# Strided value tiles loaded as 128 rows instead of 118 in a fused attention and feed-forward kernel

## The chip, the cores and the metric

The kernel runs on one core of a Trainium2 chip. Its time is device microseconds of one execution. Before the change three runs gave 945.47, 946.59 and 947.21 us, a median of 946.59 us. The profiled execution took 947.53 us; its span from the first to the last instruction is 945.7 us. All times below are counted from the start of that span.

## The reference

Attention with 8 heads over 8 sequences of 576 positions, then a feed-forward block on all 4608 tokens. Heads 0 to 3 see the last 32 keys (local), heads 4 to 7 see every 32nd key (strided):

```python
rel = pos[:, None] - pos[None, :]
mask_local = (rel >= 0) & (rel < stride)                      # stride = 32
mask_strided = (rel >= 0) & (pos[None, :] % stride == pos[:, None] % stride)
...
attn = softmax(where(mask, q @ k.T / 8, -1e9));  x = attn @ v
h = x @ w_in                                                  # 512 -> 2048
g = h * (1.0 / (1.0 + np.exp(-1.702 * h)))
return g @ w_out                                              # 2048 -> 512
```

## The kernel before

The host lays the inputs out, the core does the rest. Attention goes in 42 units, which the code calls pairs: 18 local ones (kind "l", 256 tokens each) and 24 strided ones (kind "s", eight sequences times three groups of residues). Each unit has two loads. `load_qk` (L132) brings queries and keys into a tile `qk`, of which there are two buffers. `load_v` (L140) brings values into a tile `v`, of which there are also two buffers: for a local unit 96 rows of 4096 bytes, for a strided one 118 rows of 2048 bytes. In the strided tile rows 0 to 53 are the keys of one half, rows 64 to 117 those of the other; ten rows between them are zero.

A unit then goes through six steps on the engines: `scores` (TensorE; on the trace `s` or `u`, with a small matmul from `masks_sb` ahead), `maxima` (VectorE, `nmax`), the exponentials of `softmax` (ScalarE, `pr`) and their scaling (VectorE `rinv`, GpSimd `pr`), the transposition of the probabilities (in the first nine units by TensorE into `t`, `turn_pr`, and VectorE copies into `pt_l` or `pt_s`, `fetch_pt`), `values` (TensorE, `a`, which reads `pt` and `v`), and the split of the result into a high and a low part (ScalarE `xhl`/`xhs`, VectorE `xll`/`xls`).

The feed-forward block takes 384 tokens at a time, 12 groups; each has 16 steps over slices of the hidden width. A step is 12 matmuls into `h`, an activation (`g`, `gh`, `gl`) and nine matmuls into `o`. Weights come as `raw` (two loads of 512 KB a slice) and are split by ScalarE and VectorE into `w`.

The first nine units (`n0`), numbered 0 to 8 as l, l, s, s, s, s, l, s, s, come ahead of the feed-forward steps, in the loop of L607: turn i issues the scores of unit i+1, the exponentials of unit i, the values of unit i-2 and the transposition of unit i-1. The six strided ones are the units 2, 3, 4, 5, 7, 8. The other 33 units are woven into the feed-forward steps.

The order on each engine is that of the program here. SyncE (SP) issues all loads and stores, in one queue. `load_v(i)` in turn i stands behind the values of unit i-2, whose buffer it takes; weights of the first slices stand behind it (L625, and `load_w` in L449). Each of SP's loads also waits for the load eight places ahead of it, whose semaphore it takes over.

The tracer gives nearly all instructions L116, the line of a helper, so they are told apart by tile names.

Of the kernel before, what the change touches and what calls it, by code (L numbers as in the profile page):

```python
# [18 lines left out]
P = 128  # L19
B, H, S, D = 8, 8, 576, 64  # L20
# [4 lines left out]
QB = 64  # L25
KB = QB + STRIDE
RB = 3
NB = RB * NPOS
U = 2
# [3 lines left out]
NR = (12, 10, 10)  # L33
# [14 lines left out]
HEADS = 4  # L48
# [34 lines left out]
def attn_ffn(ctx, tc, lqk, sqk, lv, sv, w_in, w_out, masks, ident, out):  # L83
# [22 lines left out]
    class InOrder:  # L106
# [17 lines left out]
    vector, scalar, gpsimd, sync = (  # L124
        InOrder(e, strict) for e in (nc.vector, nc.scalar, nc.gpsimd, nc.sync)
    )
# [3 lines left out]
    qks, vts, banks, nmaxs, exps = {}, {}, {}, {}, {}  # L130
# [9 lines left out]
    def load_v(p):  # L140
        if p < len(pairs) and p not in vts:
            kind, a, c = pairs[p]
            vts[p] = io.tile([P, 2 * U * HEADS * D], F32, tag="v", name=f"v_{p}", bufs=2)
            if kind == "l":
                sync.dma_start(out=vts[p][:KB], in_=lv[a])
            else:
                n = U * HEADS * D
                sync.dma_start(out=vts[p][: QB + NB, :n], in_=sv[a * len(NR) + c])

    warm = const.tile([P, 1], F32, name="warm")  # L150
    vector.memset(warm, 0.0)
# [428 lines left out]
    steps = [(j, f) for j, f0, f1 in spans for f in range(f0, f1)]  # L580
    load_qk(1)
    load_v(0)
    ident_sb = const.tile([P, P], F32, name="ident_sb")
    sync.dma_start(out=ident_sb, in_=ident)
# [6 lines left out]
    maxima(0)  # L591
    load_qk(2)
    load_v(1)
    load_w(0)
    halfway, valued = {}, {}
# [11 lines left out]
    for i in range(n0):  # L607
        if i + 1 < n0:
            scores(i + 1)
            load_qk(i + 3)  # L610
        if i >= 1:
            scaled(i - 1)
        if i >= 2:
            fetch_pt(i - 2)
        if i >= 3:
            late_part(i - 3)
        if i + 1 < n0:
            maxima(i + 1)
        halfway[i] = softmax(i)
        run(halfway[i], 4)  # L620
        if i >= 2:
            value_products(i - 2)
            load_v(i)
            run(valued[i - 2], 1)
        if i % 2 and i // 2 + 1 < RAWB:  # L625
            load_w(i // 2 + 1)
        weigh(i and i + 1)
        if i == n0 - 2:
            turn_pr(i - 1)
            ffn1(*steps[0], (0, 1))  # L630
        elif i == n0 - 1:
            ffn1(*steps[0], (2, 3))
            turn_pr(i - 1)
        elif i >= 1:
            turn_pr(i - 1)
# [6 lines left out]
    p = n0  # L642
# [13 lines left out]
    for s in range(len(steps) + LAG):  # L656
# [3 lines left out]
        p, q, r = due.get(s), due.get(s - 1), begins.get(s)  # L660
# [46 lines left out]
def _layout(q, k, v, w_in, w_out):  # L707
    hl = H // 2
    pad = np.zeros((B, hl, STRIDE, D), np.float32)
    kp, vp = (np.concatenate([pad, x[:, :hl]], axis=2) for x in (k, v))  # L710
    nb = S // QB

    lqk = np.zeros((NP, 2, D, 2, QKW[0] // 2), np.float32)
    lv = np.zeros((NP, KB, 2 * U, HEADS, D), np.float32)
    for i in range(NP):
        for m in range(2 * U):
            b, n = divmod(2 * U * i + m, nb)
            u, g = divmod(m, 2)
            rows = q[b, :hl, n * QB : (n + 1) * QB]
            keys = kp[b, :, n * QB : n * QB + KB]  # L720
            at = u * 2 * QB + g * QB
            lqk[i, :, :, :, at : at + QB] = rows.reshape(2, 2, QB, D).transpose(1, 3, 0, 2)
            at = QW[0] + u * (KB + QB) + g * QB
            skip = STRIDE if g and not n else 0
            lqk[i, :, :, :, at + skip : at + KB] = keys[:, skip:].reshape(
                2, 2, KB - skip, D
            ).transpose(1, 3, 0, 2)
            lv[i, :, m] = vp[b, :, n * QB : n * QB + KB].transpose(1, 0, 2)

    ns = B * len(NR)  # L730
    sqk = np.zeros((ns, 2, D, 2, QKW[1] // 2), np.float32)
    sv = np.zeros((ns, QB + NB, U, HEADS, D), np.float32)
    for i in range(ns):
        b, c = divmod(i, len(NR))
        for m in range(2 * U):
            g, u = divmod(m, U)
            r0, r1 = R0[c] + RB * m, R0[c] + min(RB * (m + 1), NR[c])
            n = (r1 - r0) * NPOS
            x = [
                y[b, hl:].reshape(hl, NPOS, STRIDE, D)[:, :, r0:r1].transpose(0, 2, 1, 3).reshape(hl, n, D)  # L740
                for y in (q, k, v)
            ]
            at = u * (NB + QB) + g * NB
            sqk[i, :, :, :, at : at + n] = x[0].reshape(2, 2, n, D).transpose(1, 3, 0, 2)
            at = QW[1] + u * 2 * NB + g * NB
            sqk[i, :, :, :, at : at + n] = x[1].reshape(2, 2, n, D).transpose(1, 3, 0, 2)
            sv[i, g * QB : g * QB + n, u] = x[2].transpose(1, 0, 2)
    lqk, sqk = (x.reshape(len(x), P, -1) for x in (lqk, sqk))
    lv, sv = (x.reshape(*x.shape[:2], -1) for x in (lv, sv))

    wi = w_in.reshape(NC, P, NF, P).transpose(2, 1, 0, 3).reshape(NF, P, DM)
    wo = w_out.reshape(NF, P, DM)
    wi, wo = (np.ascontiguousarray(x).view(np.uint64) for x in (wi, wo))
    return lqk, sqk, lv, sv, wi, wo
# [43 lines left out]
```

## Time and profile before

| | before |
|---|---|
| runs (us) | 945.47, 946.59, 947.21 |
| profiled execution / its span (us) | 947.53 / 945.7 |
| TensorE matmul busy | 913.9 us, 97% |
| VectorE / ScalarE / GpSimd busy | 476.1 / 380.6 / 53.0 us |
| DMA: moved / mean rate | 62.08 MB / 66 GB/s |
| loads of strided values | 24 of 236 KB |
| loads of strided queries and keys | 24 of 452 KB |
| loads of weights | 32 of 512 KB, two a slice |

A row of the timeline gives the start and the length of a group of instructions, then engine, operation, tile written and tiles read, how many there are, and in brackets how long the engine had been idle before it and what ended that. A row of the windows gives for a stretch the busy time of each engine, TensorE's granted clock as a share of 2.4 GHz, the mean busy share of the 16 DMA engines and their rate.

### The profile page before, as it was taken

How to read it: one execution, taken by the hardware profiler on the slowest of the kernel's cores; microseconds unless marked ns; L12 is line 12 of the kernel's file. 1: busy time of each engine (PE TensorE's matmuls, PEld its weight loads, DVE VectorE, ACT ScalarE, POOL GpSimd, SP SyncE). 2: the span in 40 equal slices, each digit the busy share in tenths (PEclk: the TensorE clock that was granted, in tenths of full speed). 3: DMA queues.
4: the chain of work that ended last, by engine and by line, in shares of the span. 5: the costliest groups of instructions: out<-in, count | busy, mean ns of one | idle time of the engine just before them, and what ended most of it. 6: DMA issues, size and time to landing. Idle time of an engine off the chain costs nothing.

```text
span 945.7 us, 16069 instructions
## 1 busy us (share of the span) xinstructions
PE 913.9 (97%) x6432; PEld 806.6 (85%) x6432; DVE 476.1 (50%) x986; ACT 380.6 (40%) x1193; POOL 53.0 (6%) x50
## 2 busy tenths in 40 slices
PE   6569999999999999999999999999999999999998
PEld 4457888888888888888888888888888888898997
DVE  3648656565454663443655564453446565322322
ACT  5649755243433442423444333332433443222221
POOL 3100001010000100000000000000000010000000
PEclk6779999999999999999999999999999999999999
DMA  8659202112112111101212120110201310000000
GB/s 262 197 164 348 97 1 90 60 41 96 35 42 84 53 53 51 45 1 64 72 50 72 52 57 34 53 38 20 80 31 43 105 29 1 34 1 1 34 1 33
DMA packets 21242, 62.08 MB, mean 66 GB/s; under 512 B 2144, under 2 KB 2400, under 8 KB 21168
## 3 DMA queue, kind: packets, MB, share of 16 engines
q1 hardware_dynamic: 21168, 61.06, 19.7%
q8 instruction: 50, 0.82, 0.4%
q14 instruction: 24, 0.20, 0.1%
HBM read 51.62 MB, written 9.44 MB: 65 GB/s over the span
## 4 chain that ended last, share of the span: by engine, by line
PE 92%; DMA 7%; DVE 0%; issue 0%; SPq 0%; ACT 0%; DVEq 0%; ACTq 0%
PE o L116 43%; PE h L116 41%; PE a L116 4%; DMA v<-sv 4%; PE s L116 3%; DMA raw<-w_out 1%; DMA qk<-sqk 1%; DMA qk<-lqk 1%; PE u L116 0%; PE t L116 0%; SPq L116 0%; ACT raw L116 0%; DVE raw L116 0%; DVE w L116 0%; DVE out L116 0%
## 5 line engine op out<-in xcount | busy, mean ns | idle before, releaser
L116 PE MATMUL o<-w,gh 128*128 128x512 f32 x1152 | 307.6, 398 | 0.0
L116 PEld LDWEIGHTS o<-w,gh 128*128 128x128 f32 x1152 | 211.1, 187 | 39.0 <-ACT gh L116 0.4
L116 PE MATMUL h<-xhl,w 128*128 128x384 f32 x768 | 229.7, 339 | 2.0 <-DVE w L116 1.4
L116 PE MATMUL h<-xhs,w 128*128 128x384 f32 x768 | 227.2, 336 | 0.0
L116 DVE SCALAR_TENSOR_TENSOR g<-g,h 128x384 f32<-128x384 f32 x192 | 106.1, 553 | 225.2 <-ACT g L116 224.6
L116 ACT ACTIVATE g<-h 128x384 f32<-128x384 f32 x192 | 93.7, 488 | 264.3 <-PE h L116 188.1
L116 PE MATMUL o<-w,gl 128*128 128x512 f32 x576 | 169.6, 395 | 0.0
L116 ACT CAST gh<-g 128x384 fp32r<-128x384 f32 x192 | 98.8, 514 | 155.2 <-DVE g L116 155.1
L116 PEld LDWEIGHTS h<-xhl,w 128*128 128x128 f32 x768 | 142.3, 188 | 12.2 <-DVE w L116 2.3
L116 DVE TENSOR_TENSOR gl<-g,gh 128x384 fp32r<-128x384 f32 x192 | 112.0, 583 | 77.6 <-ACT gh L116 76.1
L116 PEld LDWEIGHTS h<-xhs,w 128*128 128x128 f32 x768 | 141.9, 188 | 0.1
L116 PEld LDWEIGHTS o<-w,gl 128*128 128x128 f32 x576 | 107.8, 187 | 26.6
L116 PE MATMUL h<-xll,w 128*128 128x384 f32 x384 | 129.6, 338 | 0.0
L116 PE MATMUL h<-xls,w 128*128 128x384 f32 x384 | 128.7, 335 | 0.0
L116 ACT ACTIVATE pr<-pr,nmax 128x54 f32<-128x54 f32 (+1 forms) x264 | 90.3, 344 | 87.6 <-DVE nmax L116 84.6
L116 POOL TENSOR_TENSOR pr<-pr,rinv 128x432 f32<-128x432 f32 (+1 forms) x42 | 49.6, 1182 | 734.5 <-DVE rinv L116 728.0
L116 PEld LDWEIGHTS h<-xll,w 128*128 128x128 f32 x384 | 72.4, 189 | 8.8
L116 PEld LDWEIGHTS h<-xls,w 128*128 128x128 f32 x384 | 72.4, 188 | 0.0
L116 DVE STREAM_TRANSPOSE pt_l<-pr 32x256 f32<-32x256 f32 x120 | 52.2, 435 | 2.3 <-POOL pr L116 0.8
L116 DVE STREAM_TRANSPOSE pt_s<-pr 32x256 f32<-32x256 f32 x108 | 47.1, 436 | 9.5 <-POOL pr L116 8.0
L116 ACT ACTIVATION_READ_ACCUMULATOR pr<-pr,nmax 128x1 f32 x264 | 49.4, 187 | 0.0
L116 PE MATMUL a<-pt_s,v 118*64 118x108 f32 x384 | 25.3, 278 | 13.8 <-DMA v<-sv 12.2
(55 smaller groups left out, 462.3 us busy)
## 6 DMA issues: line engine op xcount, KB each, us to landing
qk<-sqk SPq DMA_DIRECT2D x24, 452.0 KB
qk<-lqk SPq DMA_DIRECT2D x17, 576.0 KB
out<-out SPq DMA_DIRECT2D x36, 256.0 KB
raw<-w_in SPq DMA_DIRECT2D x16, 512.0 KB
raw<-w_out SPq DMA_DIRECT2D x16, 512.0 KB
v<-lv SPq DMA_DIRECT2D x18, 384.0 KB
v<-sv SPq DMA_DIRECT2D x24, 236.0 KB
qk<-lqk SPq DMA_DIRECT2D x2, 288.0 KB
```

The lines of the kernel that those rows point to most:

```text
L116: ins = call(*args, **kw)
```

## The change

The host lays the strided values out as 128 rows instead of 118; rows 118 to 127 are zero. The load writes all 128 rows of the tile. The matmuls of `values` read rows 0 to 117 as before. On TensorE, VectorE, ScalarE and GpSimd the instructions and their order stay as they were. On SP the 156 rows stay in their order too, and the 24 loads `v<-sv` have the shape 128x512 instead of 118x512.

```diff
@@ load_v
             else:
                 n = U * HEADS * D
-                sync.dma_start(out=vts[p][: QB + NB, :n], in_=sv[a * len(NR) + c])
+                sync.dma_start(out=vts[p][:, :n], in_=sv[a * len(NR) + c])
@@ _layout
-    sv = np.zeros((ns, QB + NB, U, HEADS, D), np.float32)
+    sv = np.zeros((ns, P, U, HEADS, D), np.float32)
```

## Rows read from the trace of the kernel before

**Rows 1.** The page's busy times and its chain that ended last
```profile
PE 913.9 (97%) x6432; PEld 806.6 (85%) x6432; DVE 476.1 (50%) x986; ACT 380.6 (40%) x1193; POOL 53.0 (6%) x50
...
PE 92%; DMA 7%; DVE 0%; issue 0%; SPq 0%; ACT 0%; DVEq 0%; ACTq 0%
```

**Rows 2.** Windows by stage, with their columns
```profile
core 0: us, PE busy (x) PEld busy (x) DVE busy (x) ACT busy (x) POOL busy (x), PEclk, DMA share, GB/s
...
76.00:100.00 24.00, 23.27 (x126) 20.23 (x123) 19.47 (x26) 22.18 (x30) 0.00 (x0) 1.00 0.87 322
100.00:900.00 800.00, 799.96 (x5509) 711.06 (x5508) 406.61 (x841) 304.98 (x968) 39.75 (x33) 1.00 0.15 47
```

**Rows 3.** Windows (columns as in rows 2) between VectorE's copies
```profile
27.00:31.55 4.55, 2.98 (x63) 2.53 (x61) 4.35 (x12) 4.24 (x21) 0.87 (x1) 1.00 0.88 298
...
31.58:36.37 4.79, 1.33 (x36) 0.81 (x34) 4.63 (x13) 3.16 (x17) 0.91 (x1) 0.90 0.52 164
36.37:66.85 30.48, 19.13 (x190) 16.11 (x191) 10.98 (x31) 14.03 (x61) 4.20 (x4) 0.68 0.57 173
66.85:75.76 8.91, 7.07 (x52) 5.73 (x51) 7.64 (x16) 6.53 (x10) 0.00 (x0) 1.00 0.76 236
```

**Rows 4.** Chain of waits from 25 to 77 us: start, length, what
```profile
26.49 10.14 DMA v<-sv
...
38.50 15.25 DMA v<-sv
...
55.63 14.05 DMA v<-sv
```

**Rows 5.** Waits of TensorE, 25 to 77 us: us in total, times, longest
```profile
PE a L116 <- DMA v<-sv: 12.2, 4, 4.1
```

**Rows 6.** Windows (columns as in rows 2): strided load alone, store, weights
```profile
766.00:767.00 1.00, 1.00 (x7) 1.00 (x6) 0.93 (x4) 0.52 (x2) 0.00 (x0) 1.00 0.13 51
...
879.00:880.00 1.00, 1.00 (x8) 1.00 (x7) 0.00 (x0) 0.00 (x0) 0.00 (x0) 1.00 0.95 367
...
88.00:90.00 2.00, 1.79 (x10) 1.42 (x10) 1.40 (x3) 2.00 (x3) 0.00 (x0) 1.00 1.02 408
```

**Rows 7.** DMA from 762 to 769.5 us, one strided load alone
```profile
DMA packets 121, 0.26 MB, mean 34 GB/s; under 512 B 2, under 2 KB 2, under 8 KB 120
```

**Rows 8.** DMA from 878 to 881 us, two 128-row stores of 256 KB alone
```profile
DMA packets 288, 0.52 MB, mean 175 GB/s; under 512 B 32, under 2 KB 32, under 8 KB 288
```

**Rows 9.** Issues of value loads on SP, ns min/median/max
```profile
L116 SPq DMA_DIRECT2D v<-sv x24: 253/257/292, 22.2 to 762.0; - x24
L116 SPq DMA_DIRECT2D v<-lv x18: 322/332/432, 2.6 to 776.5; - x18
```

**Rows 10.** Timeline of VectorE: copies of units 3 and 7
```profile
31.58 1.51 DVE L116 COPY pt_s<-t 54x216 f32<-54x216 f32 x4
...
66.85 1.54 DVE L116 COPY pt_s<-t 54x216 f32<-54x216 f32 x4 [6.62 <-PE t L116]
```

**Rows 11.** Timeline of TensorE: products of units 3 and 8, work between
```profile
36.77 1.71 PE L116 MATMUL a<-pt_s,v 118*64 118x108 f32 x16 [3.86 <-DMA v<-sv]
38.41 1.91 PE L116 MATMUL t<-ident_sb,pr 128*54 128x128 f32 x8
40.11 0.57 PE L116 MATMUL u<-masks_sb 128*128 128x216 bf16 x2
40.60 1.12 PE L116 MATMUL u<-qk 64*64 64x54 f32 x32
...
75.76 0.96 PE L116 MATMUL a<-pt_s,v 118*64 118x108 f32 x16
```

**Rows 12.** Chain of waits: one feed-forward step in the steady stage
```profile
185.28 2.11 PE h L116 x12
187.39 2.10 PE o L116 x9
```

**Rows 13.** Window (columns as in rows 2) of the first four rows 11
```profile
36.77:41.72 4.95, 4.95 (x58) 3.81 (x58) 2.08 (x6) 3.05 (x12) 0.68 (x1) 0.50 0.54 168
```

## The prediction, made before the changed kernel was run

> **What bounds the kernel now.** The page first: TensorE is busy 913.9 of 945.7 us, and the chain that ended last is 92% TensorE and 7% DMA [rows 1]. So the kernel is at its bound nearly everywhere, and the question is where the rest lies. The windows by stage answer it: from 100 to 900 us TensorE is busy 799.96 of 800 us [rows 2]. There nothing that is done to a load can move the end. Early on it is not: 2.98 of 4.55 us from 27 us, and 19.13 of 30.48 us from 36.37 us, the latter at a mean clock of 0.68 [rows 3].
>
> The chain of waits then names the cause in this early stage: three strided value loads of 10.14, 15.25 and 14.05 us are on it [rows 4], 39.44 us in all, 4.2% of the span. TensorE's waits show the same from the other side: four times, 12.2 us in all, it sat idle ahead of value products until a `v<-sv` landed, at most 4.1 us at once [rows 5]. The idle time is much smaller than the 39 us of the chain: while the load is late TensorE finishes earlier work, and at the lower of its two clock levels.
>
> Last, why such a load is slow. One that moves alone runs at 51 GB/s with a mean DMA share of 0.13, which is 2 of 16 engines; a store of 128 such rows runs at 367 GB/s with 0.95, and weights reach 408 GB/s [rows 6]. The packets say it in another way: a strided load leaves two packets under 512 B, two 128-row stores leave 32, sixteen each [rows 7, 8]. I read these small packets as one completion write per DMA engine that takes part. So 118 rows go over two engines, 59 rows of 2048 bytes each, at some 25.5 GB/s an engine: 59 x 2048 / 25.5 GB/s = 4.7 us of moving. Every other load has a share on these two engines too, and one queued behind a strided load ends only when they are through.
>
> The Trainium skill has a rule on each side here. "DMA: Bandwidth & Descriptors" (section on why a DMA increments its semaphore by 16) says that a load uses the largest number of engines up to 16 that divides its row count: 2 for 118, 16 for 128. "SBUF — State Buffer" (section Door 1, the DMA port swizzle) says that bandwidth goes by how many of 16 ports the partitions reach; partitions 0 to 117 reach all 16 by its table, so that the change would buy nothing. The 51 GB/s speak for the first; the second is a rival below.
>
> **The change part by part.**
>
> *The load itself.* 256 KB over 16 engines at 408 GB/s is 0.64 us of moving instead of 4.7, 4 us less in an empty queue, and up to some 12 us less where earlier loads had piled up on the two engines. Unknown is whether a 128-row load spreads as the 128-row store does; the bounds are the store's 367 GB/s and the present 51. I take the store and the 128-row weights, since both sides of those transfers have the new load's row count.
>
> *The ten rows.* 24 x 20 KB more, 0.05 us each at 408 GB/s; over all 24 loads 1.2 us of DMA time, nearly all beside full TensorE work at a DMA share of 0.15 [rows 2]. If no cover hid it, 1.2 us; I count nothing.
>
> *The issue.* SP spends 257 ns on a strided load and 332 ns on a local one [rows 9]. If the new form costs what the local one does, 24 x 75 ns = 1.8 us on SP, spread over the span. SP mostly waits for TensorE, so nothing; without that cover, the six early ones are 0.45 us.
>
> *The units 2 to 8 without the wait.* Up to 36.37 us VectorE is the busy engine (4.63 of 4.79 us since the copies of unit 3 began) [rows 3, 10], and nothing that it does there waits for `v<-sv`: this stays. Then it runs dry, since TensorE, held by unit 3's values until 36.77, turns unit 4's probabilities late [rows 11]. With the values in place TensorE starts unit 3's products once the copies end (31.58 + 1.51 = 33.09), needs 0.96 us for them at full clock [rows 11], turns unit 4 by about 35, and unit 4's copies start at 36.37. From there to the copies of unit 7, three units on, the kernel now takes 30.48 us [rows 3, 10]. What is late next is one of three engines:
> - VectorE has 10.98 us of work in it [rows 3]: no earlier than 36.37 + 10.98 = 47.4.
> - ScalarE has 4.24 us per unit where it runs undisturbed (27 to 31.55 us) [rows 3]: 36.37 + 3 x 4.24 = 49.1.
> - The pace of the last undisturbed unit, 4.79 us [rows 3], gives 36.37 + 14.4 = 50.7.
>
> I take ScalarE's 49.1, since unit after unit its exponentials, casts and weight work stand in one queue and it has the most work in the whole stretch (14.03 us) [rows 3]. The copies of unit 7 then come 66.85 - 49.1 = 17.75 us sooner (16.1 to 19.5 by the other two). At full clock TensorE's own 2.98 us per unit [rows 3] fits below this.
>
> *From unit 7 to the steady stage.* From its copies to the values of unit 8 it is 8.91 us now, with VectorE busy 7.64 [rows 3]: I keep it; at most 1.3 us of it could go. From 76 to 100 us TensorE is busy 23.27 of 24 us [rows 2], so at most 0.73 us more. Weights could become late: they are wanted 18 us sooner. But the loads that stand behind the strided ones on SP come sooner by as much, and a slice of two 512 KB loads takes 2.6 us at 408 GB/s against a step of 2.11 + 2.10 us [rows 12]. I count nothing in either direction.
>
> *The other 18 strided loads.* They land while TensorE is never idle: nothing.
>
> *The queue.* A load of unit i is issued behind the values of unit i-2, so it has two units, some 8.5 us, until it is wanted. Ahead of it can stand one slice of weights and one `qk`, 1.05 + 0.46 MB, 3.7 us at 408 GB/s. It fits with some us to spare; without that spare the cost is the second rival.
>
> The sum: 947.53 - 17.75 = 929.8 on the scale of the profiled execution, whose 945.7 us of span have 1.8 us around them that stay. It was 0.94 us slower than the median of the runs; on their scale it is 928.8. I forecast 929.3, between them; 926 to 932 with the bounds above.
>
> **The rivals.**
>
> *The clock stays low.* From 36.37 to 66.85 us TensorE had a mean clock of 0.68 [rows 3], so much of the stretch at 1.2 GHz. If the early stage stays there although the waits are gone, TensorE sets the pace: 1.71 + 1.91 + 0.57 + 1.12 = 5.31 us a unit at that level [rows 11, 13], and the two half steps of the feed-forward block ahead of unit 7's transposition, 1.05 us each at full clock [rows 12], cost 4.2 us together. The copies of unit 7 come at 36.37 + 3 x 5.31 + 4.2 = 56.5, a gain of 10.3 us: 937. For it: 2.98 us busy in 4.55 is not dense work [rows 3]. Against it: in just that stretch, which the new pace resembles, the clock was 1.00 [rows 3]. The Trainium skill's "TensorE: Matmul & The Clock Gate" (Part 1) also says that idle gaps bring the clock down and work brings it up; the trace agrees (0.68 in the stretch with the gaps).
>
> *Another load is late in its place.* If the queue holds a `qk` or a `v` back by 2 us in five of the units, 10 of the 17.75 us are lost: 939. For it: DMA share 0.88 from 27 to 31.55 us [rows 3]. Against it: it moved only 298 GB/s there, and 173 GB/s in the stretch that shrinks most [rows 3]; 30.48 us of that are 5.3 MB, 13 us at 408 GB/s.
>
> *The load's spread does not change,* as the port rule would have it: then it takes as long as now, no change within 0.2%: 946.6 plus some tenths. Against it stand the 367 GB/s of the 128-row store [rows 6].
>
> *Slower.* The same rule with the added bytes on the path: if the load still moved at 51 GB/s, 20 KB more would be 0.4 us a load, and six loads in the waiting stage 2.4 us: 949. It decides if the new load alone shows 51 GB/s again. Nothing in the rows speaks for it.
>
> **How the numbers follow.** Forecast 0.68, low clock 0.18, another late load 0.07, no change 0.04, slower 0.03. The first three are faster by over 0.2% (1.9 us, about what a measurement of this kernel can tell from no change): 0.93, 0.04, 0.03. The range goes from 924.5 (19.5 us and the 1.3 and 0.73 us of the later stretches also gained, on the scale of the runs) to 937.5, which takes in the low clock; the likeliest case alone has 926 to 932.
>
> **What would show it.** Right: a strided load alone at over 300 GB/s with 16 small packets; packets under 512 B on the whole page up by 24 x 14 = 336; no `v<-sv` among TensorE's waits and none on the chain; values of unit 8 at about 58 us instead of 75.76; from 100 us on nothing but the shift. The copies of unit 7 at 49 us would confirm ScalarE's pace. Wrong: values of unit 8 later than 64 us, with a clock near 0.5 (the first rival) or a DMA named before the value or score products (the second); or an end that does not follow the early stage, with new idle time of TensorE behind 60 us.

## The result, and the profile after

The changed kernel took 931.66, 931.66, 932.41 and 933.34 us, a median of 932.03 us; beside it the kernel before took 946.03 us. The ratio is 0.9854, with a 95% interval of 0.9837 to 0.9871: 13.8 us faster, 12.2 to 15.4. The forecast was 929.3 us with a range of 924.5 to 937.5, a gain of 17.3 us on the median that was then known. The profiled execution took 931.66 us, its span is 929.8 us, 15.9 less than before.

The page's busy times, packets and chain of the changed kernel, as in [rows 1]:

```profile
PE 908.5 (98%) x6432; PEld 802.5 (86%) x6432; DVE 475.5 (51%) x986; ACT 379.6 (41%) x1193; POOL 53.0 (6%) x50
...
DMA packets 21818, 62.57 MB, mean 67 GB/s; under 512 B 2480, under 2 KB 2736, under 8 KB 21744
...
PE 95%; DMA 3%; DVE 1%; issue 0%; ACT 0%; SPq 0%; DVEq 0%
```

The DMA share of the chain fell from 7% to 3%. Before, the page had 2144 packets under 512 B: 24 x 2 + 131 x 16 of the 155 transfers. Now it has 2480 = 155 x 16, the 336 more that were forecast. (The trace has 155 loads and stores on SP; the 156 given with the change is one too many.)

One strided load alone, from 745.5 to 750 us, which answers to [rows 7]; the last column of the second line is the time from issue to landing in us:

```profile
DMA packets 145, 0.28 MB, mean 62 GB/s; under 512 B 16, under 2 KB 16, under 8 KB 144
...
v<-sv SPq DMA_DIRECT2D x1, 256.0 KB, 2.7
```

Sixteen completions instead of two, and the whole load is in after 2.7 us; before, the moving alone was 4.7 us at 51 GB/s [rows 6]. In the windows this load has 272 GB/s from 747.5 to 748.2 us, somewhat less than the 300 I had named as its sign.

The windows, columns as in [rows 2]: first between VectorE's copies of the units 3, 4, 7 and the values of unit 8, as in [rows 3], then the stretch of TensorE's longest wait, then the stages as in [rows 2]:

```profile
30.75:35.46 4.71, 3.32 (x68) 2.47 (x58) 4.55 (x13) 4.71 (x25) 0.91 (x1) 1.00 0.87 277
35.46:52.79 17.33, 11.41 (x132) 9.79 (x133) 10.40 (x32) 12.07 (x56) 4.19 (x4) 0.80 0.78 259
43.10:47.89 4.79, 0.13 (x1) 0.03 (x1) 3.08 (x7) 2.58 (x17) 1.81 (x2) 0.76 0.83 226
52.79:61.24 8.45, 7.05 (x52) 5.73 (x51) 7.64 (x16) 6.37 (x9) 0.00 (x0) 1.00 0.69 245
60.00:84.00 24.00, 23.96 (x132) 21.30 (x132) 21.21 (x30) 23.57 (x32) 0.00 (x0) 1.00 0.95 340
84.00:884.00 800.00, 799.97 (x5509) 711.18 (x5508) 406.63 (x841) 304.39 (x968) 39.70 (x33) 1.00 0.14 47
```

The stretch that took 30.48 us takes 17.33. In the stretch of the wait the DMA engines were busy 0.83 of the time and moved only 226 GB/s, not the 408 with which the prediction reckons; why the rate fell is not shown. The steady stage is as it was: 799.97 of 800 us.

TensorE's waits over the whole span, the longest first (us in total, times, longest), to be read against [rows 5]:

```profile
PE a L116 <- DMA v<-lv: 4.7, 1, 4.7
PE a L116 <- DVE pt_s L116: 3.2, 6, 1.2
PE s L116 <- DMA qk<-sqk: 1.6, 1, 1.6
```

No `v<-sv` is left among them. But one wait for a local value load is, and it is longer than any that went. It is not new: from 25 to 77 us the kernel before had it too, one row below the one shown in [rows 5]:

```profile
PE a L116 <- DMA v<-lv: 3.1, 1, 3.1
```

The chain of waits of the changed kernel has it as its only DMA from 24 to 62 us, where it had the three of [rows 4]:

```profile
38.01 9.74 DMA v<-lv
```

TensorE's timeline has the value products of the units 6 and 8, against [rows 11]:

```profile
47.89 1.97 PE L116 MATMUL a<-pt_l,v 96*64 96x64 f32 x32 [4.66 <-DMA v<-lv]
...
61.24 0.96 PE L116 MATMUL a<-pt_s,v 118*64 118x108 f32 x16
```

And VectorE's copies of the units 3, 6 and 7, against [rows 10]:

```profile
30.75 1.51 DVE L116 COPY pt_s<-t 54x216 f32<-54x216 f32 x4
...
42.95 1.23 DVE L116 COPY pt_l<-t 96x512 f32<-96x512 f32 x2
...
52.79 1.55 DVE L116 COPY pt_s<-t 54x216 f32<-54x216 f32 x4 [6.57 <-PE t L116]
```

Unit 7's copies came at 52.79 us; the forecast had 49.1. Unit 6's products also read the copies of unit 6, which ended at 44.18 us, so the load alone held them for the last 3.7 of the 4.66 us. What stood ahead of that one local load is seen on SP from 33 to 42 us (start, length of the issue, what):

```profile
33.30 0.33 SPq L116 DMA_DIRECT2D v<-sv  x1
33.68 0.43 SPq L116 DMA_DIRECT2D raw<-w_in  x1
34.16 0.42 SPq L116 DMA_DIRECT2D raw<-w_out  x1
34.62 0.43 SPq L116 DMA_DIRECT2D raw<-w_in  x1
35.10 0.43 SPq L116 DMA_DIRECT2D raw<-w_out  x1
35.62 0.54 SPq L116 DMA_DIRECT2D qk<-lqk  x1
38.01 0.33 SPq L116 DMA_DIRECT2D v<-lv  x1
...
```

Two slices of weights (3 and 4, 2.1 MB) and a local query load (unit 9's, 0.59 MB) go out within 2.5 us, behind a strided load of 0.26 MB. That is 2.9 MB, 7.2 us at 408 GB/s and longer at the lower rate that was measured, and unit 6's values queue behind it.

### The profile page after: what moved, and what is told of

Same layout as the page of the kernel before. It is cut to its first block, busy times and chain, and to the rows that moved or that the text cites. A ratio compares the mean times of both kernels' runs of the same rounds, so it can differ in the third digit from the quotient of the medians.

```text
span 929.8 us, 16069 instructions
## 1 busy us (share of the span) xinstructions
PE 908.5 (98%) x6432; PEld 802.5 (86%) x6432; DVE 475.5 (51%) x986; ACT 379.6 (41%) x1193; POOL 53.0 (6%) x50
## 2 busy tenths in 40 slices
DMA packets 21818, 62.57 MB, mean 67 GB/s; under 512 B 2480, under 2 KB 2736, under 8 KB 21744
## 4 chain that ended last, share of the span: by engine, by line
PE 95%; DMA 3%; DVE 1%; issue 0%; ACT 0%; SPq 0%; DVEq 0%
PE o L116 44%; PE h L116 43%; PE a L116 4%; PE s L116 3%; DMA v<-lv 1%; DMA qk<-sqk 1%; DMA qk<-lqk 1%; DVE pt_s L116 0%; PE t L116 0%; PE u L116 0%; DVE w L116 0%; DVE nmax L116 0%; SPq L116 0%; ACT w L116 0%; DVE rinv L116 0%
## 5 line engine op out<-in xcount | busy, mean ns | idle before, releaser
L116 DVE TENSOR_SCALAR rinv<-ssum 128x8 f32<-128x8 f32 x42 | 7.1, 169 | 58.2 <-ACT pr L116 58.0
```

What stands on the lines that cost most here:

```text
L116: ins = call(*args, **kw)
```

## Experiments

Theory A: a load goes over as many DMA engines as its row count allows by division; 118 allows two, and the six strided loads of the early stage held TensorE up. Its rivals: the ports that the partitions reach, the bytes, or padding as such; or that the later 18 loads have a part in it. Theory B, on the miss of the forecast: the 4.7 us wait is queueing, and what is in the queue can be moved. Its rival: the engines set the pace, and the wait is only where that shows.

### Other row counts

```diff
-                sync.dma_start(out=vts[p][:, :n], in_=sv[a * len(NR) + c])
+                sync.dma_start(out=vts[p][:122, :n], in_=sv[a * len(NR) + c])
-    sv = np.zeros((ns, P, U, HEADS, D), np.float32)
+    sv = np.zeros((ns, 122, U, HEADS, D), np.float32)
```

Expected of 122 rows:

> 122 rows instead of 128, the last four zero. Theory (the row count sets how many DMA engines share a load; 122 = 2 x 61, so two engines): as before the change, 945 to 949 us, two packets under 512 B for each strided load, 2144 on the page, a v<-sv among TensorE's waits with about 12 us. Rival (the number of SBUF ports that the partitions reach, or the total of bytes, sets it; or padding as such helps): like the changed kernel, 930 to 934 us.

Measured: 947.48 us, ratio to before 1.0012 (1.0003 to 1.0022). Packets of the page and TensorE's waits from 24 to 80 us:

```profile
DMA packets 21338, 62.28 MB, mean 66 GB/s; under 512 B 2144, under 2 KB 2400, under 8 KB 21264
```

```profile
PE a L116 <- DMA v<-sv: 9.8, 4, 4.7
```

Two completions a load again, and four waits again, 9.8 us in all where about 12 were expected. Four rows of padding bought nothing.

Expected of 120 rows, the same edit with 120:

> 120 rows, the last two zero. Theory (120 = 15 x 8, so fifteen engines): like the changed kernel within 2 us, 930 to 935 us, 15 completion packets for each strided load (24 x 15 + 131 x 16 = 2456 under 512 B on the page). Rival (only a full tile of 128 rows is spread): as before, 945 to 949 us.

Measured: 932.6 us, ratio 0.985 (0.9831 to 0.9869), the changed kernel's time. The page has 24 x 15 + 131 x 16 packets:

```profile
DMA packets 21602, 62.18 MB, mean 67 GB/s; under 512 B 2456, under 2 KB 2712, under 8 KB 21528
```

Fewer rows than 122, and the whole gain: it is neither the padding nor the number of rows. The completions are 2, 15 and 16 for 122, 120 and 128 rows, which is the largest number up to 16 that divides each. So the Trainium skill states it in "DMA: Bandwidth & Descriptors" (section on why a DMA increments its semaphore by 16), and these runs agree. "SBUF — State Buffer" (section Door 1, the DMA port swizzle) has all 16 ports for 118, 120 and 122 rows alike; for this case that does not decide, by 947.48 against 932.6 us.

### Early loads alone, late loads alone

```diff
-                sync.dma_start(out=vts[p][:, :n], in_=sv[a * len(NR) + c])
+                r = P if p < n0 else QB + NB
+                sync.dma_start(out=vts[p][:r, :n], in_=sv[a * len(NR) + c, :r])
```

Expected of 128 rows in the six early loads alone:

> 128 rows in the six strided loads of the first nine units, 118 in the other 18. Theory (all of the gain comes from the early stage, where TensorE waits): 930 to 934 us, ratio to before 0.985 as with all 24. Rival (the later loads help too, through the stores and query loads that queue behind them): 936 us or more, with the rest of the gain missing.

Measured: 930.48 us, ratio 0.983 (0.9811 to 0.9849). The interval overlaps that of the changed kernel: nothing of the gain is missing.

Expected of the complement (`r = QB + NB if p < n0 else P`):

> The complement: 118 rows in the six early strided loads, 128 in the other 18. Theory: no gain, 945 to 948 us, within 0.2% of before, although the later loads land some 4 us sooner. Rival (later loads matter): 1 to 8 us faster than before.

Measured: 946.91 us, ratio 1.0011 (0.9999 to 1.0022). Issues of strided loads (the last number of the first line is the median from issue to landing; for loads over two engines the profile gives none, so that the 4 us of the expectation cannot be read) and the steady stage:

```profile
v<-sv SPq DMA_DIRECT2D x18, 256.0 KB, 3.4
v<-sv SPq DMA_DIRECT2D x6, 236.0 KB
```

```profile
100.00:900.00 800.00, 799.98 (x5510) 711.27 (x5509) 405.62 (x839) 302.76 (x965) 39.71 (x33) 1.00 0.14 47
```

Eighteen loads that land after 3.4 us are worth nothing where TensorE is never idle. The whole gain is the six early ones'.

### What stands ahead of unit 6's values

The query loads of the units 9 and 10, which the first nine units do not need, go behind the value loads of the units 6 and 7:

```diff
             scores(i + 1)
-            load_qk(i + 3)
+            if i + 3 < n0:
+                load_qk(i + 3)
...
             load_v(i)
+            if n0 <= i + 3 < n0 + 2:
+                load_qk(i + 3)
```

> Changed kernel, with the query loads of the units 9 and 10 (not needed until the feed-forward steps) issued behind the value loads of the units 6 and 7 instead of ahead of them. Theory (the 4.7 us that TensorE waits for the local values of unit 6 are queueing behind earlier loads, and make up the miss of the forecast): one load of 1.4 us leaves the queue ahead of them, the wait falls to about 3.2 us, 930 to 931.5 us. Rival (the pace of the early stage is set by the engines and the wait is only where it shows): no change, 932 us.

Measured: 928.99 us, ratio 0.9818 (0.9796 to 0.9839), somewhat better than expected, with an interval that reaches to 931.5 us and just touches that of the changed kernel. The profiled execution took 932.34 us. The wait in it, and its window from the copies of unit 4 to those of unit 7:

```profile
47.85 1.98 PE L116 MATMUL a<-pt_l,v 96*64 96x64 f32 x32 [3.69 <-DMA v<-lv]
```

```profile
35.30:52.93 17.63, 12.78 (x132) 10.62 (x133) 10.53 (x31) 12.31 (x56) 4.20 (x4) 0.74 0.83 267
```

The wait is 1.0 us shorter than with the query load ahead (4.66), where theory B had 1.4 us, but the stretch is no shorter (17.63 against 17.33 us). The same wait also differs where the order of the loads is the changed kernel's. With 128 rows in the early loads alone, and with 120 rows:

```profile
46.73 1.98 PE L116 MATMUL a<-pt_l,v 96*64 96x64 f32 x32 [3.09 <-DVE rinv L116]
```

```profile
48.33 1.98 PE L116 MATMUL a<-pt_l,v 96*64 96x64 f32 x32 [5.65 <-DMA v<-lv]
```

(The first names a `rinv` that ended just before; it belongs to unit 8, and unit 6's products do not read it.) So 3.69 us lies within what the old order gives, and this run alone does not decide between theory B and its rival.

Then slice 4 of the weights as well, whose loads are kept back until unit 8's value load is out (the tile is taken where it was):

```diff
         raw = raws[f] = w_tile([P, 2, DM, 2], U32, f"raw_{f}")
-        for m in range(2):
-            sync.dma_start(out=raw[:, m], in_=(w_in, w_out)[m][f])
+        held[f] = raw
+        if f not in (4,):
+            send_w(f)
...
+            if i == 8:
+                send_w(4)
```

> As qk_behind, and the two weight loads of slice 4 issued behind the value load of unit 8. Theory: 1.4 + 2.6 us of queue leave, the wait falls from 4.7 to under 1 us, the copies of unit 7 come at 48 to 49 us as was forecast, 926.5 to 928.5 us; the clock drop that follows the wait goes as well. Rival (engines set the pace): 931 to 932 us. Second rival (slice 4 is late in its place): a wait for weights of 1 us or more at its scaling, 930 us or more.

Measured: 925.96 us, ratio 0.978 (0.9765 to 0.9795), the lowest median of all kernels here, clear of the changed one by the ratios to the kernel before, and 0.5 us below the range expected. All of TensorE's waits from 24 to 80 us; VectorE's copies of the units 3, 4 and 7; windows between the copies of 3, 4 and 7, and one of low clock:

```profile
PE a L117 <- DVE pt_s L117: 2.6, 4, 1.2
PE h L117 <- ACT w L117: 0.7, 1, 0.7
PE h L117 <- DVE w L117: 0.6, 1, 0.6
PE a L117 <- DVE pt_l L117: 0.3, 1, 0.3
```

```profile
29.72 1.51 DVE L117 COPY pt_s<-t 54x216 f32<-54x216 f32 x4
34.43 1.51 DVE L117 COPY pt_s<-t 54x216 f32<-54x216 f32 x4
...
46.61 1.54 DVE L117 COPY pt_s<-t 54x216 f32<-54x216 f32 x4 [0.89 <-PE t L117]
```

```profile
29.72:34.43 4.71, 3.32 (x69) 2.47 (x58) 4.55 (x13) 4.71 (x25) 0.91 (x1) 1.00 0.97 352
34.43:46.61 12.18, 10.75 (x132) 8.95 (x133) 10.62 (x31) 11.36 (x55) 4.01 (x4) 0.86 0.75 258
...
36.98:40.40 3.42, 3.42 (x46) 2.63 (x48) 2.93 (x11) 3.41 (x18) 1.47 (x1) 0.50 0.86 290
```

No wait for a DMA is left. From the copies of unit 3 to those of unit 7 it is 16.89 us; the forecast had 49.1 - 31.58 = 17.5, the changed kernel has 22.04. The three units behind the copies of unit 4 take 4.06 us each, where the forecast had 4.24. So the time per unit was near the forecast's, and the miss was the wait. The rival with the engines falls. That ScalarE sets this pace is not shown: it was busy 11.36 of 12.18 us, but VectorE 10.62 and TensorE 10.75. Two parts of the expectation were missed: the copies of unit 7 came at 46.61, not 48 to 49 us (those of unit 3 came at 29.72, 1.86 us before the 31.58 of the forecast), and the low clock did not all go, with 0.50 (1.2 GHz) from 36.98 to 40.40 us although no wait for a DMA stood ahead of it.

Slice 3 behind unit 6's values as well (`send_w(3)` at i == 6):

> As qk_w4_behind, and the weight loads of slice 3 issued behind the value load of unit 6. Theory: the queue ahead of unit 6's values is empty, but under 1 us of wait was left: 926 to 928.5 us, at most 1 us better than qk_w4_behind. Rival (slice 3 is late in its place, since it is scaled behind the values of unit 6): 1 to 3 us slower than qk_w4_behind.

Measured: 926.2 us, ratio 0.9783 (0.9768 to 0.9797): no difference from the last one. The queue was short enough already, and slice 3 is not late either.

Last, the order of the run before that one (query loads behind, slice 4 kept back), but 118 rows:

> The order of qk_w4_behind with 118 rows, as before the change. Theory (the two clogged engines hold the early stage): four of the five waits stay, the long one for the loads of unit 5 and 6 shortens at most; 940 to 946 us. Rival (the order alone would have done it, 118 rows or not): 930 us or less.

Measured: 948.13 us, ratio to before 1.0017 (1.0007 to 1.0027). This expectation was missed: not 940 to 946 but a little slower than before. The profiled execution took 946.67 us. The chain of waits from 22 to 82 us has two DMAs, TensorE waits for unit 8's values, and it waits for weights from 72 to 84 us:

```profile
37.04 14.71 DMA v<-sv
...
59.48 14.14 DMA raw<-w_out
```

```profile
71.38 1.55 PE L117 MATMUL a<-pt_s,v 118*64 118x108 f32 x16 [2.54 <-DMA v<-sv]
```

```profile
PE h L117 <- DVE w L117: 1.7, 1, 1.7
PE h L117 <- ACT w L117: 1.0, 1, 1.0
```

With 118 rows the strided loads still need 14.71 us, and the weights that were kept back take 14.14 us behind them. The copies of unit 7 came 6.4 us sooner (60.45 us against 66.85 of [rows 10]). Some of that was gone at unit 8's values, which had to wait for their strided load and came 4.4 us sooner (71.38 against 75.76 of [rows 11]); most of the rest went behind them, where the late weights are. The spans differ by 0.8 us. So this order alone is no gain; it is one only where the two engines are not clogged.

## Why the prediction was right, and where it was off

*The bound and the cause.* Right. The steady stage did not move (799.96 and 799.97 of 800 us), the late loads alone gave nothing, the early ones alone all of it. Two engines for 118 rows are shown by 122 and 120 rows, against the rival with the ports. The rival with more bytes on the path falls with them.

*The load itself.* Right: sixteen completions, 2.7 us to landing, though 272 GB/s are below the sign that was named.

*The issue.* The bound was right. SP's issue of a strided load went from a median of 257 to 328 ns, to just what the local loads take [rows 9], and cost nothing that the runs show: all 24 loads and the early six give the same time within their intervals.

*The pace of the units.* 4.24 us per unit were forecast, 4.06 us measured where no load was late. That ScalarE is what sets it stays argued.

*The queue.* This step failed in its size. "Ahead of it can stand one slice of weights and one `qk`", 3.7 us, was right for the units 2 to 5 and 8, whose loads landed 2.6 to 4.9 us after their issue in the changed kernel, but not for the local unit 6 and the unit 7 behind it (9.74 and 8.48 us): turn 5 issues slice 3 (L625) and also slice 4 (L449), and turn 6 a local query load, which is larger than the strided one. With 2.9 MB in the queue, unit 6's values took 9.74 us to land and TensorE waited 4.66 us. This is the second rival, which had 0.07 and a price of 10 us: one wait of 4.7 us in place of five of 2 us. The order of the loads on SP had all that was needed to see it; I summed the queue for a typical unit and not for each of the seven. The waits of before had it as well: TensorE stood 3.1 us ahead of unit 6's values there, and the forecast let this wait go with the four strided ones without a reason of its own. It did not go but grew, by 1.6 us.

*The clock.* The first rival did not come true: 1.00 from 30.75 to 35.46 us. In the one long wait the clock fell to 1.2 GHz and stayed there to 52.42 us, which is the mean of 0.80:

```profile
45.60:52.42 6.82, 4.53 (x41) 4.20 (x42) 0.58 (x3) 2.00 (x4) 0.91 (x1) 0.50 0.45 142
```

It had been as low after the first of the waits of before [rows 13].

*The later stretches.* I had bounded them at 1.3 and 0.73 us and counted nothing. From the copies of unit 7 to the values of unit 8 it is 8.45 instead of 8.91 us, 0.5 gained. TensorE's idle time from 76 to 100 us, 0.73 us before, is 0.04 us from 60 to 84 us now. So the two small gains that I had left out came, 1.2 us in all.

The account in the two profiled executions: the copies of unit 7 came 14.06 us sooner, 3.7 less than forecast. Of the 4.66 us of wait, 0.83 us is made up by an earlier start (unit 3's copies at 30.75 instead of 31.58 us). The strided loads need not have had a part in that, since the two executions were already further apart before the first of them was issued (unit 0's values began at 20.17 and 18.88 us); I take it for the scatter of the first 20 us, which no run here tells apart from a cause. With 1.2 us of later gains this is 15.3 of the 15.9 us by which the spans differ; 0.6 us stays without a place. The medians differ by 13.8 us.

One sum of the range was off: 946.59 less 19.5, 1.3 and 0.73 us is 925.1, not 924.5. Nothing hangs on it.

## What to carry to other kernels

Look at the completions and the DMA share of a load that moves alone before its rate is taken for granted: a row count with no large divisor up to 16 can be padded, by two rows here, for fifteen engines instead of two. When a clogged queue is cleared, sum anew what stands ahead of every single load that something waits for, not of a typical one; the longest queue left sets the next wait. Loads that nothing waits for yet go behind those that something will.

## What the runs showed of the hardware that was not expected

The two engines held up loads that have shares on all sixteen. In the trace of the kernel before, 14 of the 16 completions of the weight load issued at 38.81 us were in by 43.58 us; the last two came at 54.95 and 56.00 us.

SP itself stood still meanwhile. Two issues on SP's timeline of the kernel before, between 32 and 44 us:

```profile
32.99 3.07 SPq L116 DMA_DIRECT2D qk<-sqk  x1
...
40.11 3.42 SPq L116 DMA_DIRECT2D raw<-w_out  x1
```

An issue that otherwise takes 0.33 to 0.43 us took over 3 us there. In the changed kernel the same two loads were issued in 0.33 and 0.42 us. The longest issue of any load there is 1.34 us. In all four kernels whose early strided loads go over two engines, SP's issue of one weight load near 40 us took 3.39 to 3.47 us; in the other six no issue took over 1.49 us. Why SP is held is not shown by any run here.
